# High and low parts of the last 64 attention rows formed at the scaling of the units; a new order of the end; the first block's combinations in two sections

## The chip, the cores and the metric

The kernel runs on one core of one Trainium2 chip. The core has five engines that this document speaks of by the profile's names: PE (TensorE, matrix products; PEld is its weight load), DVE (VectorE), ACT (ScalarE), POOL (GpSimd) and SP (SyncE), which here only issues DMAs. The metric is the time of one execution on the device in microseconds, the median of the runs. Lower is better.

## The reference

A transformer-like block with a gate. S = 2048 tokens, D = 576, 32 heads of 18, F = 4608, all in float32:

```python
def _A_ref(x, wqkv, wo):                     # attention
    qkv = (x @ wqkv).reshape(B, S, 3, H, Dh).transpose(2, 0, 3, 1, 4)
    q, k, v = qkv[0], qkv[1], qkv[2]
    p = _softmax(jnp.einsum("bhqd,bhkd->bhqk", q, k) * (Dh ** -0.5), axis=-1)
    o = jnp.einsum("bhqk,bhkd->bhqd", p, v)
    return o.transpose(0, 2, 1, 3).reshape(B, S, D) @ wo

def _B_ref(x, w_gate, w_up, w_down):         # feed-forward
    return (_gelu(x @ w_gate) * (x @ w_up)) @ w_down

x = A_x
xn = _layernorm(x, axis=-1)
s = _A_ref(xn, A_wqkv, A_wo)
g = _silu(_B_ref(xn, B_w_gate, B_w_up, B_w_down))
return x + s * g
```

## The kernel before

**High and low parts.** Matrix products that have to be accurate are made of two reduced-precision parts of each operand: `hi` is the value rounded to the matmul's type, `lo` is what is left (`cut`, lines 436 to 441). A product then takes three matmuls: hi times hi, hi times lo, lo times hi.

**Sections.** The feed-forward part is cut into 144 sections, S0 to S143: for each of 4 blocks of 512 tokens, 18 groups r of 256 hidden columns, in two halves. A section is 27 pairs of matmuls (gate and up, L412). Into 128 sections the attention is spliced: scores for the row maxima (`pm`, L780, reduced on DVE, L782), scores again and their exponentials (`pe`, L832, and ACT L833), and the sums of values (`acc`, L849). Small pieces of work for other engines hang on a section's pair numbers as hooks. The splits of the next section's weights (`wh`, `wl`, L110 and L112, three pairs of instructions on POOL) are made while a section runs.

**Downs.** After the two halves of a group comes a down projection, `down`: seven products of a Strassen-like scheme into PSUM tiles `py` (L523), of which DVE adds each to one of seven sums M in SBUF (L530). The tiles pg/pu, pm, pe, py and po of PE share a few PSUM buffers (`ring`: three), so PE waits where an older tile isn't read yet. The weight operand T of a down (high and low, seven slots each) is formed on chip once and stored; later downs load it in four pieces (`t_piece`, 576 and 432 KB). For the first group of a block M is not added to but copied: on DVE for the second block (L526), on ACT for the third and fourth (L528). After a block's last down the seven sums are combined in four pairs of in-place operations (`COMBINED`, L542), and four of them, the block's quarters, are stored to `ys` (L549).

**Attention's outputs** are scaled in 32 units u = 8j + g (token block j, head group g): a unit is loaded, multiplied by the reciprocals of its sums on POOL (L693) and stored to `on[j]`, 576 rows, in four DMAs (L700).

**The end.** The 576 attention rows are projected with `wo` in 16 steps of 128 tokens. A step k is `project` (28 matmuls, L1006), `multiply` (the gate and the sum with x, L1015 to L1020, and the store L1021) and `split_o(k + 2)`, which forms the operands of a later step: `oh` on ACT from all five row groups (128x640, L989), `ol` on DVE from the first four (L990), and for the last 64 rows their low part on DVE into the upper half of `oh`'s fifth slot (L991). The fifth slot then holds high rows over low rows. `split_wo` forms `wo`'s two parts, `woh` on ACT (L968) and `wol` on POOL (L966, L970). The raw `wo` lies in the tiles xx and yy, which later hold rows of x and of y. The attention rows of a block lie in KA (`load_o`: 1024 KB, L718, and 128 KB, L719). The last sections are mixed with the steps by hand. D0, D1 and D2 are the last three downs (`last_down`):

```python
# order on PE: S139, S140, S141, D0, steps 0 to 3, S142, steps 4 to 6, D1, step 7, S143,
#              steps 8 to 10, D2, step 11, gates of the last block with steps 12, then 13 to 15
```

**What sets the order.** PE's and SP's instructions stand in the order of the code in the whole program. SP issues its DMAs one after the other, and one that waits for its source or for its buffer holds up those behind it. On ACT, DVE and POOL a scheduler sets the order, up to the end, from where on (`manual_schedule`) it is that of the code too. Each engine takes its instructions in that order.

Of the kernel before, what the change touches and what calls it, by code (L numbers as in the profile page):

```python
# [8 lines left out]
F32 = mybir.dt.float32  # L9
F32R = mybir.dt.float32r  # L10
# [55 lines left out]
def f(ap):  # L66
    return ap.bitcast(F32)
# [15 lines left out]
def kernel(ctx: ExitStack, tc: tile.TileContext, x, wqkv, wo, w_gate, w_up, w_down, out):  # L83
# [12 lines left out]
    rT = dram.tile([H, S], F32, name="rT")  # L96
    on = [dram.tile([D, TB], F32, name=f"on{b}") for b in range(NB)]
    mxT = [dram.tile([8 * QD, P], F32, name=f"mxT{i}") for i in range(2)]
# [5 lines left out]
    ident = const.tile([P, P], F32, name="ident")  # L104
    make_identity(nc, ident)
    all_t = slice(0, TB)

# [406 lines left out]
    def down(b, r, then={}):  # L514
        if b == 0 and r < PLAIN:
            return down_plain()
        (ah, al), T, M = FF["A"], FF["T"], FF["M"]
        for m, (i, k) in PRODUCTS:
            py = ring("py")
            for t in range(2):  # L520
                tt = slice(t * P, (t + 1) * P)
                for n, (h, w) in enumerate(((ah, 0), (ah, 1), (al, 0))):
                    nc.tensor.matmul(py[:, t, 0:DC], h[:, i, tt], T[:, w, k], start=n == 0, stop=n == 2)  # L523
            if r == 0:
                if b == 1:
                    nc.vector.tensor_copy(M[:, m], py[:, :, 0:DC])  # L526
                else:
                    nc.scalar.activation(M[:, m], py[:, :, 0:DC], AF.Copy)  # L528
            else:
                nc.vector.tensor_tensor(M[:, m], py[:, :, 0:DC], M[:, m], op=ALU.add)  # L530
            for eng, to, op, by in then.get(m, ()):
                eng.tensor_tensor(M[:, to], M[:, to], M[:, by], op=op)
        if r == NR - 1 and b < NB - 1:
            FF["gates"].append(b)
            one = nc.vector if b == 0 else nc.gpsimd
            for i, p, q in COMBINED:
                FF["hooks"].setdefault(i, []).append(lambda p=p, q=q: (combine(one, *p), combine(nc.gpsimd, *q)))

    def combine(eng, to, op, by):

        M = FF["M"]
        tc.keep_in_program_order(eng.tensor_tensor(M[:, to], M[:, to], M[:, by], op=op))  # L542

    def gates():

        for b in FF["gates"]:
            for i, c, m in QUARTERS:
                rows = slice(b * TB + TH * i, b * TB + TH * i + TH)
                nc.sync.dma_start(ys[rows, DC * c:DC * c + DC].rearrange("(t p) d -> p t d", p=P), FF["M"][:, m])  # L549
        FF["gates"] = []  # L550
# [139 lines left out]
    def scale(u, i):  # L690

        o, d = (t[:, i, 0:TB] for t in SC)
        nc.gpsimd.tensor_tensor(o, o, d, op=ALU.mult)  # L693

    def store_scale(u, i):

        j, g = divmod(u, NQ)
        for a in range(QD):
            row = (QD * g + a) * DH
            nc.sync.dma_start(on[j][row:row + DH, :], SC[0][32 * a + 1:32 * a + 1 + DH, i, 0:TB])  # L700

# [13 lines left out]
    def load_o(b):  # L715

        i = OTS[b]
        nc.sync.dma_start(f(KA)[:, i:i + KT], on[b][0:R0, :].rearrange("(k p) t -> p k t", p=P))  # L718
        nc.sync.dma_start(f(KA)[0:HR, i + KT], on[b][R0:D, :])  # L719

    ctx.enter_context(tc.manual_schedule(engines={mybir.EngineType.SP}))

    with tc.tile_pool(name="att", bufs=1, reuse_waits="tile") as att:
        VS = [att.tile([P, VC * VW + 32 - DH - 1], F32, name=f"VS{i}") for i in range(VB)]
        for i, kk in enumerate(KS):
            for r in range(2):
                (nc.vector, nc.gpsimd)[i % 2].memset(f(kk[r]), 1.0)
# [218 lines left out]
    with tc.tile_pool(name="epi", bufs=1, reuse_waits="tile") as epi:  # L946
# [37 lines left out]
        def split_o(k):  # L984
            if k < len(groups):
                b, j = groups[k]
                oh, ol = OP[k] = [epi.tile([P, c, P], F32R, name=m, bufs=2) for m, c in (("oh", NK), ("ol", KT))]
                raw = f(KA)[:, OTS[b]:OTS[b] + NK, j * P:(j + 1) * P]
                act.activation(oh, raw, AF.Copy)  # L989
                vec.tensor_tensor(ol, raw[:, 0:KT], f(oh)[:, 0:KT], op=SUB)  # L990
                vec.tensor_tensor(oh[HR:P, KT, :], raw[0:HR, KT], f(oh)[0:HR, KT, :], op=SUB)  # L991

        def gate(k):
            if gated <= k < len(groups) and groups[k][0] < NB - 1:
                yy = YY[k % len(YY)]
                th = epi.tile([P, D], F32, name="th")
# [3 lines left out]
        def project(k):  # L1000
            po = ring("po")
            oh, ol = o = OP.pop(k)
            terms = [(c, i, w) for c in range(KT) for i, w in ((0, 0), (0, 1), (1, 0))] + [(KT, 0, 0), (KT, 0, 1)]
            for c in range(2):
                for m, (i, a, w) in enumerate(terms):
                    nc.tensor.matmul(po[:, c, 0:DC], o[a][:, i, :], OW[w][:, i, DC * c:DC * c + DC], start=(m == 0),  # L1006
                                     stop=(m == len(terms) - 1))
            return po
# [13 lines left out]

        def step(ahead=True):
            nonlocal n
            multiply(n, project(n))
# [10 lines left out]
            if ahead:  # L1036
                gate(n + 1)

# [3 lines left out]
        def last_section(tag):  # L1042
# [16 lines left out]
            t1 = h[:, 0:2].rearrange("p a t -> p (a t)")  # L1059
            act.activation(t1, pg, AF.Square)  # L1060
            vec.scalar_tensor_tensor(t1, t1, 1.0 / GC, pg, op0=ADD, op1=ALU.mult)
            act.activation(t1, t1, AF.Tanh, scale=GC * GS)

            def end():
# [3 lines left out]
            return h, end  # L1068

# [9 lines left out]
        load_raw(first + 2)  # L1079
        h, end = last_section("f")  # L1080
        todo.pop("rec")[0]()
# [10 lines left out]
        h, end = last_section("ring")  # L1092
# [12 lines left out]
        end()  # L1105
        gate(0)
        gate(1)
        sums_a(0, h, pool)
# [10 lines left out]
        for k in range(3, len(XX)):  # L1119
            load_x(k)  # L1120
        for k in range(4):
            step()
        h, end = last_section("ring")
        end()
        for k in range(2):
            step()
        step(False)
        last_down(1)
        gate(n + 1)
        sums_a(0, h, pool)  # L1130
        cut_a(0, h, pool, pool)
        step()
        h, end = last_section("f")
        end()
        sums_a(1, h, vec)
        cut_a(1, h, act, vec)
        for k in range(2):
            step()
        step(False)
        last_down(2, {6: ((vec, 6, SUB, 3),), 0: ((vec, 6, ADD, 0), (pool, 5, ADD, 0), (pool, 5, ADD, 2)),  # L1140
                      4: ((vec, 6, SUB, 4), (vec, 4, ADD, 2)), 1: ((pool, 5, SUB, 1), (pool, 1, SUB, 3))})
        step()
        M = FF["M"]
        for i, c, m in QUARTERS:
            t = ffn.tile([P, 2, DC], F32, name="tg", tag=("h0", "h1")[c], bufs=2 - c)
            act.activation(t, M[:, m], AF.Tanh, scale=0.25)
            vec.scalar_tensor_tensor(M[:, m], t, 1.0, M[:, m], op0=ADD, op1=ALU.mult)
            if m == 4:
                step()
        for k in range(3):  # L1150
            step()
# [28 lines left out]
```

## Time and profile before

| | us |
|---|---|
| median of 3 runs | 2583.61 (2580.03 to 2584.37) |
| the profiled execution's own time | 2580.15 |
| its span, first to last instruction | 2578.4 |
| PE busy | 2545.5 (99%) |
| DVE busy | 2105.1 (82%) |
| POOL busy | 1630.5 (63%) |
| ACT busy | 1464.1 (57%) |

The rows of the trace are to be read so. A row of a timeline is: start and duration in us, engine, line, operation, output and inputs, shapes, count; in square brackets is the engine's idle time just before and what ended it. The chain of waits lists, in order of time, the pieces of work that decide the end: start, duration, engine, what, line. A row of the stretches gives for each engine its busy time and the number of its instructions, then the granted clock of PE (1.00 is full), the mean busy share of the 16 DMA engines and the rate in GB/s. All numbers below are of the one profiled execution.

### The profile page before, as it was taken

Reading aid. Unit: us, or ns where it says so; the run is one execution under the profiler, and the core shown is the slowest. Engines: PE = TensorE matmul, PEld = TensorE weight load, DVE = VectorE, ACT = ScalarE, POOL = GpSimd, SP = SyncE. Lnnn points to the kernel's source line nnn. Section 1 sums busy time; section 2 is a strip of 40 time slices with the busy share of each in tenths; the row PEclk is TensorE's granted clock in tenths of the full one; section 3 lists DMA queues with packets and bytes.
Section 4 is the critical chain, followed back from the end, with each engine's and each line's share of the span. In section 5 each row is a group of like instructions: output and inputs, shape, how many; then the busy total and the mean of one; then the engine's idle time right before and its main releaser. Section 6 shows DMA issues by size and latency. Waiting matters only on the chain.

```text
span 2578.4 us, 52876 instructions
## 1 busy us (share of the span) xinstructions
PE 2545.5 (99%) x20548; PEld 1838.7 (71%) x20548; DVE 2105.1 (82%) x2383; ACT 1464.1 (57%) x1765; POOL 1630.5 (63%) x1692
## 2 busy tenths in 40 slices
PE   9999999999999999999999999999999999999988
PEld 8888766676766676666667766666776766666787
DVE  5325888888889888888888888889887888897467
ACT  3224366666666655555666555656656556666621
POOL 2105588888888856566658566666657566666662
PEclk9999999999999999999999999999999999999999
DMA  8854455555575566666686666666668656665684
GB/s 259 270 187 131 104 165 163 163 166 167 163 197 177 164 157 163 166 162 166 169 195 182 168 172 168 167 164 170 166 162 210 165 159 165 165 164 148 174 264 138
DMA packets 409769, 446.43 MB, mean 173 GB/s; under 512 B 106924, under 2 KB 286636, under 8 KB 409520
## 3 DMA queue, kind: packets, MB, share of 16 engines
q1 hardware_dynamic: 409520, 443.04, 62.8%
q8 instruction: 164, 2.69, 0.5%
q14 instruction: 85, 0.70, 0.1%
HBM read 347.07 MB, written 95.85 MB: 172 GB/s over the span
## 4 chain that ended last, share of the span: by engine, by line
PE 95%; DVE 3%; DMA 1%; ACT 1%; POOL 1%; issue 0%; SPq 0%; DVEq 0%; POOLq 0%; ACTq 0%
PE pg L412 26%; PE acc L849 18%; PE py L523 15%; PE pm L780 9%; PE pe L832 9%; PE pu L412 8%; PE po L189 7%; PE po L1006 1%; PE py L510 1%; PE pt L250 0%; DVE mx L782 0%; DMA yy<-in_A_wo_dram 0%; DVE ol L990 0%; DVE M L530 0%; DMA od<-rT 0%
## 5 line engine op out<-in xcount | busy, mean ns | idle before, releaser
L833 ACT ACTIVATE pT<-pe 128x1024 f32<-128x1024 f32 x1024 | 1047.7, 1027 | 578.0 <-PE pe L832 542.6
L782 DVE TENSOR_REDUCE mx<-pm 128x2 f32<-128x1024 f32 x1024 | 1220.9, 1224 | 167.5 <-PE pm L780 151.9
L412 PE MATMUL pu<-xd,wh 64*128 64x512 f32 x2538 | 925.6, 396 | 1.6 <-DVE t L426 1.6
L412 PE MATMUL pg<-xd,wh 64*128 64x512 f32 x2538 | 924.8, 396 | 1.9 <-ACT t L425 1.9
L412 PEld LDWEIGHTS pg<-xd,wh 64*128 64x128 f32 x2538 | 467.7, 184 | 122.4 <-issue 57.9
L412 PE MATMUL pg<-xd,wl 64*128 64x512 f32 x1269 | 495.4, 390 | 1.2 <-POOL wl L117 1.2
L412 PE MATMUL pu<-xd,wl 64*128 64x512 f32 x1269 | 495.1, 390 | 0.0
L412 PEld LDWEIGHTS pu<-xd,wh 64*128 64x128 f32 x2538 | 467.5, 184 | 20.4 <-DVE t L426 2.9
L849 PE MATMUL acc<-pT,VS 128*32 128x512 f32 x4096 | 466.0, 595 | 0.0
L110 POOL TENSOR_SCALAR wh<-raw 128x384 fp32r<-128x384 f32 x402 | 215.9, 539 | 381.4 <-PE pu L412 272.5
L112 POOL TENSOR_TENSOR wl<-raw,wh 128x384 fp32r<-128x384 f32 x402 | 414.1, 1032 | 28.4
L780 PE MATMUL pm<-KA,QT 64*128 64x512 f32 x2048 | 414.1, 394 | 4.6 <-ACT pT L833 2.8
L832 PE MATMUL pe<-QT,KA 64*128 64x512 f32 x2048 | 410.1, 392 | 3.3 <-DVE mx L782 3.3
L523 PE MATMUL py<-T,ah 128*128 128x288 f32 x1876 | 382.8, 299 | 7.6 <-DVE M L530 7.5
L530 DVE TENSOR_TENSOR M<-py,M 128x576 f32<-128x576 f32 x448 | 338.7, 758 | 30.4 <-PE py L523 17.6
L523 PEld LDWEIGHTS py<-T,ah 128*128 128x128 f32 x1876 | 299.8, 189 | 62.5 <-issue 54.0
L441 POOL TENSOR_TENSOR al<-h,ah 128x512 fp32r<-128x512 f32 (+1 forms) x142 | 292.5, 2060 | 52.6 <-ACT ah L438 42.4
L849 PEld LDWEIGHTS acc<-pT,VS 128*32 128x32 f32 x4096 | 120.2, 109 | 276.6 <-issue 229.6
L523 PE MATMUL py<-T,al 128*128 128x288 f32 x938 | 276.5, 295 | 0.0
L832 PEld LDWEIGHTS pe<-QT,KA 64*128 64x128 f32 x2048 | 192.7, 184 | 113.8 <-DVE mx L782 28.4
L412 PEld LDWEIGHTS pg<-xd,wl 64*128 64x128 f32 x1269 | 234.0, 184 | 37.4 <-POOL wl L117 2.0
L412 PEld LDWEIGHTS pu<-xd,wl 64*128 64x128 f32 x1269 | 234.2, 185 | 9.6
(163 smaller groups left out, 2925.4 us busy)
## 6 DMA issues: line engine op xcount, KB each, us to landing
T<-ts SPq DMA_DIRECT2D x98, 576.0 KB
KA<-qk SPq DMA_DIRECT2D x768, 72.0 KB
T<-ts SPq DMA_DIRECT2D x98, 432.0 KB
raw<-in_B_w_gate_dram SPq DMA_DIRECT2D x144, 288.0 KB
raw<-in_B_w_up_dram SPq DMA_DIRECT2D x144, 288.0 KB
ts<-T SPq DMA_DIRECT2D x36, 576.0 KB
VS<-vs SPq DMA_DIRECT2D x128, 152.0 KB
qk<-t SPq DMA_DIRECT2D x72, 256.0 KB
```

The source lines that it names most:

```text
L110: first = nc.gpsimd.tensor_scalar(hi, raw, 1.0, 1.0, op0=ALU.mult, op1=ALU.mult)
L112: keep(nc.gpsimd.tensor_tensor(lo, raw, f(hi), op=ALU.subtract))
L189: nc.tensor.matmul(o, st, m, start=(i == 0), stop=(i == len(terms) - 1))
L412: nc.tensor.matmul(o, w[1 + wp][k][rr, c, :], xd[k][xp][rr, c, :], start=(i == 0), stop=(i == len(terms) - 1))
L441: keep(two.tensor_tensor(lo, raw, f(hi), op=ALU.subtract))
L523: nc.tensor.matmul(py[:, t, 0:DC], h[:, i, tt], T[:, w, k], start=n == 0, stop=n == 2)
L530: nc.vector.tensor_tensor(M[:, m], py[:, :, 0:DC], M[:, m], op=ALU.add)
L780: nc.tensor.matmul(pm[:, a], QS[u, r][rr, t * P:(t + 1) * P], KS[(u * NA + c) % KB][r][rr, :], start=True, stop=True)
L782: return nc.vector.tensor_reduce(MX[u][:, 2 * r:2 * r + 2, t, c], pm, axis=AX.X, op=ALU.max)
L832: nc.tensor.matmul(pe[:, a], KS[(u * NA + c) % KB][r][rr, t * P:(t + 1) * P], QS[u, r][rr, :], start=True, stop=True)
L833: nc.scalar.activation(PT[u, kt][:, 2 * r:2 * r + 2, :], pe, AF.Exp, scale=SCALE)
L849: nc.tensor.matmul(ACC[u][32 * a:32 * a + 32, :], VS[(u * NA + c) % VB][:, v:v + 32], pt[:, a, :], start=first, stop=last, skip_group_chec ...
```

## The change

It has four parts.

1. **The last 64 rows.** `on[j]` gets 640 rows. In the units that hold the last 64 attention rows (g = 7, four of 32) POOL forms their high part, with a mask `split_rows` that is 0 for the rows of the first 512, and subtracts it (L706 and L707 of the changed kernel). Nine DMAs store high and low rows one after the other, where four stored the rows. `load_o` then brings the fifth slot with both parts, 256 KB for 128 KB, and `project` reads it from KA. `split_o` forms four groups only: ACT 128x512 for 128x640, and L991 is gone.
2. **The first block.** Its four pairs of combinations, which stood in the one section after the block's last down, are spread: one in that section, three in the next; its stores to `ys` go later too. The seven copies of M for the second block go from DVE to ACT.
3. **The order of the end.** PE's order becomes S139, S140, S141, D0, steps 0 to 2, S142, 3 to 5, D1, S143, 6 to 8, D2, 9 to 15. `split_wo` and `split_o(1)` are issued behind D0. The gelu of a section (all of it) is issued in one piece after it or after the first step behind it. In the half `cut_a(1)` of S143 the low part goes from DVE to POOL.
4. **Loads and shares.** `load_o(2)` and `load_o(3)` are issued with steps 3 and 7, where they were issued with 1 and 5. POOL takes the addition of x in odd steps below 8, before below 11.

The core of the diff:

```diff
-SHARED = 11
+SHARED = 8
-COMBINED = ((6, (6, ADD, 0), (5, ADD, 0)), (12, (6, SUB, 3), (5, ADD, 2)), (18, (6, SUB, 4), (5, SUB, 1)),
-            (24, (4, ADD, 2), (1, SUB, 3)))
+COMBINED = (((6, ADD, 0), (5, ADD, 0)), ((6, SUB, 3), (5, ADD, 2)), ((6, SUB, 4), (5, SUB, 1)), ((4, ADD, 2), (1, SUB, 3)))
...
             if r == 0:
-                if b == 1:
-                    nc.vector.tensor_copy(M[:, m], py[:, :, 0:DC])
-                else:
-                    nc.scalar.activation(M[:, m], py[:, :, 0:DC], AF.Copy)
+                nc.scalar.activation(M[:, m], py[:, :, 0:DC], AF.Copy)
...
-            for i, p, q in COMBINED:
-                FF["hooks"].setdefault(i, []).append(lambda p=p, q=q: (combine(one, *p), combine(nc.gpsimd, *q)))
+            if b == 0:
+                combine_at(14, nc.vector, *COMBINED[0])
+            else:
+                for k in range(4):
+                    combine_at(6 * k + 6, nc.gpsimd, *COMBINED[k])
...
+            if b == 0:
+                for i, k in ((2, 1), (8, 2), (13, 3)):
+                    combine_at(i, nc.vector, *COMBINED[k])
+                FF["hooks"].setdefault(20, []).append(lambda b=b: store_gates(b))
+            else:
+                store_gates(b)
...
         nc.gpsimd.tensor_tensor(o, o, d, op=ALU.mult)
+        if u % NQ == NQ - 1:
+            nc.gpsimd.tensor_scalar(d.bitcast(F32R), o, split_rows, 1.0, op0=ALU.mult, op1=ALU.mult)
+            nc.gpsimd.tensor_tensor(o, o, d, op=SUB)
...
-        nc.sync.dma_start(f(KA)[0:HR, i + KT], on[b][R0:D, :])
+        nc.sync.dma_start(f(KA)[:, i + KT], on[b][R0:R0 + P, :])
...
-                vec.tensor_tensor(ol, raw[:, 0:KT], f(oh)[:, 0:KT], op=SUB)
-                vec.tensor_tensor(oh[HR:P, KT, :], raw[0:HR, KT], f(oh)[0:HR, KT, :], op=SUB)
+                vec.tensor_tensor(ol, raw, f(oh), op=SUB)
...
-            b, j = groups[min(n + 2, len(groups) - 1)]
+            b, j = groups[n]
             if b < 2 and j == TB // P - 1:
                 load_o(b + 2)
...
+        h1, gelu = last_section("f")
+        last_down(0)
         split_wo()
-        split_o(1)
         for k in range(3):
             load_x(k)
         for k in range(2, 4):
             load_y(k)
-        h1, end = last_section("f")
-        last_down(0)
-        end()
-        gate(0)
-        gate(1)
+        split_o(1)
+        gelu()
...
         last_down(1)
-        gate(n + 1)
         sums_a(0, h, pool)
         cut_a(0, h, pool, pool)
+        h, gelu = last_section("f")
+        gelu()
+        sums_a(1, h, vec)
+        for k in range(3):
+            step()
+            if k == 0:
+                cut_a(1, h, act, pool)
+        last_down(2, {0: ((pool, 5, ADD, 0), (pool, 5, ADD, 2)),
...
-        h, end = last_section("f")
-        end()
-        sums_a(1, h, vec)
-        cut_a(1, h, act, vec)
-        for k in range(2):
-            step()
-        step(False)
```

Three places show what moves.

POOL between S140 and D0, before: the scaling of the last two units, `wol`, and then the three splits of S142's weights (raw_31111), of which the first stands last here.

```order
L693 TENSOR_TENSOR on_11642<-on_11642,od_11643 128x512 x2
L966 MEMSET wol_31010 64x576
L970 TENSOR_TENSOR wol_31010<-xx0_31011,woh_31009 128x576
L970 TENSOR_TENSOR wol_31010<-xx1_31012,woh_31009 128x576
L970 TENSOR_TENSOR wol_31010<-xx2_31013,woh_31009 128x576
L970 TENSOR_TENSOR wol_31010<-yy2_31016,woh_31009 128x576
L970 TENSOR_TENSOR wol_31010<-yy3_31017,woh_31009 64x576
L110 TENSOR_SCALAR wh_31232<-raw_31111 128x384
L112 TENSOR_TENSOR wl_31233<-raw_31111,wh_31232 128x384
```

And now (raw_31140 are S142's raw weights; a third pair L110, L112 stands between the last row of the first part and the first of the second):

```order
L704 TENSOR_TENSOR on_11653<-on_11653,od_11654 128x512 x2
L706 TENSOR_SCALAR od_11654<-on_11653,split_rows_87 128x512
L707 TENSOR_TENSOR on_11653<-on_11653,od_11654 128x512
L110 TENSOR_SCALAR wh_31249<-raw_31140 128x384
L112 TENSOR_TENSOR wl_31250<-raw_31140,wh_31249 128x384
L110 TENSOR_SCALAR wh_31253<-raw_31140 128x384
L112 TENSOR_TENSOR wl_31254<-raw_31140,wh_31253 128x384
```

and, behind that third pair,

```order
L991 MEMSET wol_31042 64x576
L995 TENSOR_TENSOR wol_31042<-xx0_31043,woh_31041 128x576
L995 TENSOR_TENSOR wol_31042<-xx1_31044,woh_31041 128x576
L995 TENSOR_TENSOR wol_31042<-xx2_31045,woh_31041 128x576
L995 TENSOR_TENSOR wol_31042<-yy2_31048,woh_31041 128x576
L995 TENSOR_TENSOR wol_31042<-yy3_31049,woh_31041 64x576
```

All of `wol` now stands behind the three splits, and each of these reads S142's raw weights.

SP from step 6's end on, before: step 7's store is that of xx0_31011, step 8's that of xx1_31012, and the load of KA for the last block (on3_72) has gone after step 5.

```order
L1021 DMA out_0_dram<-xxs_31372 128x576
L978 DMA yy2_31016<-ys_75 128x576
L982 DMA xxs_31372<-in_A_x_dram 128x576
L1021 DMA out_0_dram<-xx0_31011 128x576
L468 DMA T_1911<-ts_77 128x1152
L468 DMA T_1911<-ts_77 128x864
L978 DMA yy3_31017<-ys_75 128x576
L982 DMA xx0_31011<-in_A_x_dram 128x576
L1021 DMA out_0_dram<-xx1_31012 128x576
L468 DMA T_1911<-ts_77 128x1152
L468 DMA T_1911<-ts_77 128x864
```

And now: step 6's store is that of xxs_31409, step 7's that of xx0_31043.

```order
L1047 DMA out_0_dram<-xxs_31409 128x576
L468 DMA T_1912<-ts_77 128x1152
L468 DMA T_1912<-ts_77 128x864
L1003 DMA yy2_31048<-ys_75 128x576
L1007 DMA xxs_31409<-in_A_x_dram 128x576
L1047 DMA out_0_dram<-xx0_31043 128x576
L740 DMA KA_1913<-on3_72 128x4x512
L741 DMA KA_1913<-on3_72 128x512
L468 DMA T_1912<-ts_77 128x1152
L468 DMA T_1912<-ts_77 128x864
```

The load of KA (1024 and 256 KB) now stands between the two halves of T, and both it and T's second half stand behind the store of step 7.

DVE in the section after the first block's last down and at the start of the next, before (L782 are the reductions of the maxima, L422 to L429 the first section's gelu):

```order
L542 TENSOR_TENSOR M_1908<-M_1908 128x576
L782 TENSOR_REDUCE mx_8414<-pm_9156 128x2
L782 TENSOR_REDUCE mx_8414<-pm_9172 128x2
L542 TENSOR_TENSOR M_1908<-M_1908 128x576
L782 TENSOR_REDUCE mx_8414<-pm_9194 128x2
L542 TENSOR_TENSOR M_1908<-M_1908 128x576
L782 TENSOR_REDUCE mx_8414<-pm_9210 128x2
L782 TENSOR_REDUCE mx_8414<-pm_9226 128x2
L542 TENSOR_TENSOR M_1908<-M_1908 128x576
L782 TENSOR_REDUCE mx_8414<-pm_9244 128x2
L422 SCALAR_TENSOR_TENSOR h1_9254<-h1_9254,pg_9100 128x512
L426 TENSOR_TENSOR t2_9257<-t2_9257,pg_9100 128x512
```

with no combination in the section behind. And now in the section behind, while one combination is left in the first:

```order
L905 RECIPROCAL sums_8833<-sums_8833 128x16
L807 TENSOR_REDUCE mx_9327<-pm_9328 128x2
L544 TENSOR_TENSOR M_1909<-M_1909 128x576
L807 TENSOR_REDUCE mx_9327<-pm_9347 128x2
L544 TENSOR_TENSOR M_1909<-M_1909 128x576
L827 STREAM_TRANSPOSE mt_9362<-m2_9275 128x32
L807 TENSOR_REDUCE mx_9327<-pm_9366 128x2
L807 TENSOR_REDUCE mx_9327<-pm_9385 128x2
L544 TENSOR_TENSOR M_1909<-M_1909 128x576
```

Of four combinations on DVE three have moved behind the gelu of the first section, in among the next section's reductions. On POOL their partners moved likewise, the last one behind the three sums that form `tsum` (L475 to L477).

More of the change, by code (lines that the diff above doesn't have):

```diff
@@ L96 @@
     rT = dram.tile([H, S], F32, name="rT")
-    on = [dram.tile([D, TB], F32, name=f"on{b}") for b in range(NB)]
+    on = [dram.tile([R0 + P, TB], F32, name=f"on{b}") for b in range(NB)]
     mxT = [dram.tile([8 * QD, P], F32, name=f"mxT{i}") for i in range(2)]
@@ L724 @@
         VS = [att.tile([P, VC * VW + 32 - DH - 1], F32, name=f"VS{i}") for i in range(VB)]
+        nc.gpsimd.memset(split_rows, 1.0)
+        for c in range(1 + R0 % DH):
+            nc.gpsimd.tensor_tensor(split_rows, split_rows, ident[:, c:c + 1], op=SUB)
         for i, kk in enumerate(KS):
@@ L1021, in multiply, with step @@
             nc.sync.dma_start(out[rows(k), :], xx)
-        def step(ahead=True):
+        def step():
             nonlocal n
-            multiply(n, project(n))
+            po = project(n)
+            multiply(n, po)
             split_o(n + 2)
-            b, j = groups[min(n + 2, len(groups) - 1)]
+            b, j = groups[n]
             if b < 2 and j == TB // P - 1:
@@ L1091 @@
         split_o(0)
-        h, end = last_section("ring")
-        end()
+        h, gelu = last_section("ring")
+        gelu()
         for i, u in enumerate(rest):
@@ L1147 @@
             vec.scalar_tensor_tensor(M[:, m], t, 1.0, M[:, m], op0=ADD, op1=ALU.mult)
-            if m == 4:
+            for k in range({6: 1, 4: 2}.get(m, 0)):
                 step()
-        for k in range(3):
+        for k in range(2):
             step()
```

71 lines of the change are left out of this document (41 added, 30 removed).

## The prediction

> **What bounds the kernel now.** I read the page's busy times first, then in the timeline of PE the rows that end its idle times, then the chain of waits back from the longest.
>
> ```profile
> PE 2545.5 (99%) x20548; PEld 1838.7 (71%) x20548; DVE 2105.1 (82%) x2383; ACT 1464.1 (57%) x1765; POOL 1630.5 (63%) x1692
> ```
>
> PE is the bound: idle 32.9 us of a span of 2578.4. The change takes no matmul away, so all it can win or lose are waits of PE. Those at its places:
>
> ```profile
> 761.24 0.50 PE L832 MATMUL pe<-QT,KA 64*128 64x512 f32 x2 [1.03 <-DVE mx L782]
> 765.28 0.50 PE L832 MATMUL pe<-QT,KA 64*128 64x512 f32 x2 [1.21 <-DVE mx L782]
> 767.73 0.50 PE L832 MATMUL pe<-QT,KA 64*128 64x512 f32 x2 [1.03 <-DVE mx L782]
> 2476.19 0.85 PE L523 MATMUL py<-T,ah 128*128 128x288 f32 x2 [5.58 <-DVE M L530]
> 2491.45 0.40 PE L1006 MATMUL po<-woh,oh 128*128 128x288 f32 x1 [1.12 <-DVE oh L991]
> 2518.88 0.53 PE L523 MATMUL py<-T,ah 128*128 128x288 f32 x2 [1.26 <-DVE M L530]
> 2542.35 0.40 PE L1006 MATMUL po<-woh,ol 128*128 128x288 f32 x1 [2.05 <-DVE ol L990]
> 2549.45 0.53 PE L523 MATMUL py<-T,ah 128*128 128x288 f32 x2 [0.66 <-DVE M L530]
> 2562.18 0.40 PE L1006 MATMUL po<-woh,ol 128*128 128x288 f32 x1 [1.25 <-DVE ol L990]
> ```
>
> The idle time before a row stands in its brackets, with what ended it. Three rows at the first change of blocks, 3.27 us, behind DVE; six at the end, 5.58 + 1.12 + 1.26 + 2.05 + 0.66 + 1.25 = 11.9 us. Where the 5.58 comes from, the chain of waits tells:
>
> ```profile
> 2461.44 8.69 DMA yy<-in_A_wo_dram
> ...
> 2471.56 1.79 DVE ol L990
> ...
> 2476.19 5.12 PE py L523 x24
> 2481.31 3.73 PE po L1006 x28
> ...
> 2518.88 3.47 PE py L523 x24
> ```
>
> `split_o(1)` stands ahead of D0's additions on DVE and waits for `wo`. The 24 matmuls after the stall took 5.12 us, after the short wait at 2518.88 as many took 3.47: a restart after a long wait costs 1.65 more.
>
> **The change, part by part.** Work that no wait of PE hangs on: two POOL instructions and five more DMAs in each of four units lie in idle time of POOL (37% of the span) and of SP, except at the end, where POOL's are counted. The nearest rows for them:
>
> ```profile
> L440 POOL TENSOR_SCALAR ah<-h 128x512 fp32r<-128x512 f32 x2 | 1.7, 835 | 2.0 <-PE py L523 1.9
> L441 POOL TENSOR_TENSOR al<-h,ah 128x512 fp32r<-128x512 f32 x2 | 2.6, 1284 | 0.2
> ```
>
> 2.1 us together. ACT, which gets the shorter split, is busy 57%.
>
> *The end of D0 and step 0.* With `split_o(1)` behind D0 the 5.58 goes, and PE is at step 0 at 2470.61 + 24 x 0.133 (3.73/28) = 2473.8. What is late next is `wol`, which step 0's second matmul reads.
>
> ```profile
> 2448.20 0.63 SPq L130 DMA_DIRECT2D raw<-in_B_w_up_dram  x1
> 2454.06 0.52 POOL L110 TENSOR_SCALAR wh<-raw 128x384 fp32r<-128x384 f32 x1 [0.63 <-DMA raw<-in_B_w_up_dram]
> 2467.96 0.64 SPq L130 DMA_DIRECT2D raw<-in_B_w_up_dram  x1
> 2467.98 0.58 POOL L966 MEMSET wol<- 64x576 f32 x1
> 2468.64 4.17 POOL L970 TENSOR_TENSOR wol<-xx,woh 128x576 fp32r<-128x576 f32 x3
> 2475.99 0.51 POOL L110 TENSOR_SCALAR wh<-raw 128x384 fp32r<-128x384 f32 x1
> 2480.69 0.74 POOL L447 TENSOR_TENSOR h<-h 128x256 f32<-128x256 f32 x1
> ```
>
> Now the three splits stand ahead, and wait for S142's weights, issued as before up to 2467.96. The load of S141's took 5.9 us from issue (2448.20) to the split that waited for it (2454.06); as much here gives 2473.9. It is 2475.99 at the latest, where the split began without a wait; and POOL isn't through with the scaling before 2467.9 (where the memset began) + 2.1 = 2470.0. I take 2473.9. Splits 2480.69 - 2475.99 = 4.7, memset 0.66, `wol` 2475.99 - 2468.64 = 7.35: the first part of `wol` is there at 2480.6, the last at 2486.6, and step 0 needs some 15 more matmuls (2.0, and 15/24 of the 1.65 for a restart, 1.0): its end is 2489.6 against 2485.04. **+4.6**; from the two bounds -0.4 to +7.3.
>
> ```profile
> 2479.00:2480.00 1.00, 1.00 (x6) 1.00 (x6) 0.52 (x1) 0.00 (x0) 0.92 (x3) 0.54 0.89 244
> 2480.00:2481.00 1.00, 1.00 (x9) 1.00 (x9) 0.68 (x2) 0.00 (x0) 1.00 (x2) 1.00 0.98 332
> ```
>
> These stretches show the restart: the granted clock (before the DMA share) is still 0.54 in the fourth us after the stall, then 1.00. The Trainium skill (TensorE: Matmul & The Clock Gate, Part 1: The HAM clock gate) says that full clock comes back only after about 3.4 us of sustained activity; the trace agrees for a dense restart. By that rule step 0, which would get a few matmuls each time a part of `wol` is formed, would not count as busy, and some of step 1 would run slowly too: up to 0.7 more than my 1.0. No row shows such a drip.
>
> *The waits after it.* L991 is gone, D0's additions stand ahead of the splits and nothing new stands ahead of the later ones: 1.12 + 1.26 + 2.05 + 0.66 + 1.25 = **-6.3**. If one of the larger stays for another reason, -4.
>
> *D2.* Its second matmul reads T's second half. In the chain at S143:
>
> ```profile
> 2532.41 0.05 PE pg L412
> ...
> 2537.44 1.28 ACT ah L438
> L441 POOL TENSOR_TENSOR al<-h,ah 128x1280 fp32r<-128x1280 f32 x1 | 3.2, 3246 | 0.1
> L1020 POOL TENSOR_TENSOR xx<-xx,yy 128x576 f32<-128x576 f32 x3 | 5.6, 1867 | 23.3 <-DVE yy L1015 22.3 <-DMA xxs<-in_A_x_dram 1.0
> PEld py L523 <- DMA T<-ts: 0.3, 1, 0.3
> 2542.11 0.93 SPq L468 DMA_DIRECT2D T<-ts  x2
> 2497.00:2503.00 6.00, 6.00 (x53) 4.90 (x53) 2.86 (x3) 0.74 (x1) 4.34 (x5) 1.00 1.03 355
> 2542.00:2546.00 4.00, 3.65 (x27) 3.61 (x27) 3.89 (x6) 0.00 (x0) 1.82 (x1) 1.00 0.84 268
> ```
>
> S143 ends at 2532.47, its high part is ready 6.25 us later. POOL then makes the low part (3.25), and its addition of x in step 7 stands behind that (1.87): step 7's store can go 11.4 us after S143. PE is through its three steps after 3 x 3.73 = 11.2. SP issues behind that store the load of KA and only then T's second half. Bytes up to T's first needed piece: 288 + 1024 + 256 + 576 KB, 2.2 MB, at 355 GB/s (the stretch where KA was loaded) 6.2 us. The pair of pieces issued at 2542.11, 1.03 MB, was through at about 2546, 3.9 us, of which 2.9 are its bytes at that rate: about 1 us from issue to the first bytes. Landing 11.4 + 0.3 + 6.2 + 1.0 = 18.9 after S143. PE waits **7.7**, and 1.65 for its restart: **+9.3**. The lower bound: the piece isn't held up by KA. Then it is issued 12.7 after S143 (KA's two issues and the store's before it) and has the 3.9 us: 16.6, a wait of 5.4. The upper bound has everything at 268 GB/s and T's whole pair waited for, 2.6 MB in 9.8 us: 11. With the restart 5 to 13. I take the first, since the piece stands in the one queue of SP right behind KA, and 16 engines busy 1.03 in that stretch leave it no free way. The Trainium skill (DMA: Bandwidth & Descriptors, Queues, rings and completion order) has it that each DMA engine takes one issuer's descriptors in order; by this the piece comes behind KA and the wait is the 7.7, without it the 5.4. No row here has a piece of T close behind a load of KA.
>
> *The first block.*
>
> ```profile
> L528 ACT ACTIVATE M<-py x14: 651/652/654, 1387.8 to 1992.8; 128x576 f32<-128x576 f32 x14
> L542 DVE TENSOR_TENSOR M<-M x4: 1200/1408/1847, 758.6 to 768.7; 128x576 f32<-128x576 f32 x4
> 768.50:782.50 14.00, 14.00 (x122) 8.78 (x120) 13.60 (x17) 10.06 (x12) 12.00 (x14) 1.00 0.90 257
> 788.20 0.80 POOL L477 TENSOR_TENSOR tsum<-rawd 128x288 f32<-128x288 f32 x1
> 789.93 1.17 ACT L483 ACTIVATE T<-tsum 128x1152 fp32r<-128x1152 f32 x1 [4.73 <-PE py L523]
> 793.29 1.94 ACT L833 ACTIVATE pT<-pe 128x1024 f32<-128x1024 f32 x2 [0.34 <-PE pu L412]
> ```
>
> The first section loses three of four combinations on DVE: of its 3.27 some 2.1 go, or all. The second section had 13.60 of 14.00 us of DVE busy, one combination of 1.20 in it; with three (median 1.41, 4.2) it has 16.6, so PE waits about 2.5 (1.0 if what DVE carried over shrinks with the first section, 3.9 if they take 1.85). DVE's seven copies behind it go to ACT, 7 x 0.65 = 4.6 us. ACT had 4.73 idle, but now waits: M1's last combination stands on POOL behind the sums ending 789.0, its store follows it (789.0 + 1.4 + 0.8 for 288 KB and 1 to start: 792 at best, 793 with what stands in SP's queue), and only then may M1 be copied; the exponentials that began at 793.29 stand behind that copy, L483 and two more splits, at about 796.6. PE has three buffers; I take 2.5 of these 3.3, bounds 0 and 3.3. Sum -2.1 + 2.5 + 2.5 = **+2.9**; -2.3 to +5.1.
>
> Sum: 4.6 - 6.3 + 9.3 + 2.9 = **+10.5** on 2580.15, 2590.7. That execution lies at the lower end of the runs, 3.5 below their median; on the median it would be 2594.1. I forecast 2593.
>
> **Rivals.** (a) D2 doesn't wait. For it: in before T's pieces were waited for once, 0.3 us, and a load of KA moves only 128 KB more than before. Against it: the order on SP and POOL. It decides at 11.2 us after S143, and 9.3 falls away: +1.2, 2581 on the profiled execution. This one ends on the other side, not slower. (b) The weights land early and the block change pays: step 0 at -0.4 and the blocks at -2.3, with D2 as forecast: +0.3, 2580. Against it stands the load of 5.9 us. Only (a) and (b) together are faster: -9, 2571. (c) The change doesn't do what it says: the later waits stay in part and the bounds of step 0 and D2 lie high: -4 + 7.3 + 13 + 2.9 = +19, 2599 (2603 on the median).
>
> **How the numbers follow.** Forecast, +5.2 to +15: 0.68; (c) 0.13; (a) 0.08 and (b) 0.05, of which a part still falls outside 0.2%; both 0.06. A measurement of this kernel can tell about 0.2%, 5.2 us, from no change. Slower 0.82, same 0.11, faster 0.07. The range runs from (a) and (b) on the median, 2584, less a little, to (c): 2583 to 2603.
>
> **What would show it.** Right: no wait at the first matmuls of D0's third product, a wait of some 7 us at step 0's second matmul ended by POOL `wol`, and one of some 8 at D2's first product ended by the DMA of T; new waits behind DVE in 770 to 785 and behind ACT after 787. Wrong: `wol` before 2474, or T's second half landing before D2.

## The result and the profile after

The changed kernel takes 2599.7 us in the median of 4 runs (2598.63 to 2600.66), the one before 2583.29 in the runs beside them. The ratio is 1.0066, with a 95% interval of 1.0048 to 1.0083: slower, by 12 to 21 us.

The page of the changed kernel, its busy times and its chain by engine:

```profile
PE 2553.1 (98%) x20548; PEld 1846.2 (71%) x20548; DVE 2083.8 (80%) x2360; ACT 1465.4 (56%) x1772; POOL 1642.1 (63%) x1710
PE 92%; POOL 2%; DMA 2%; DVE 1%; issue 1%; ACT 1%; SPq 0%; POOLq 0%; DVEq 0%; ACTq 0%
```

The matmuls are as many. The span of the profiled execution is 2598.9, 20.5 longer than that of before, with 12.9 us more idle time of PE (2598.9 - 2553.1 against 32.9) and 7.6 more in which it was busy, at a lower clock as will be seen. DVE has 21 us less to do, and POOL and DMA hold 2% of the chain each, where they held 1%. The rows of PE's timeline in the changed kernel that end a wait, at the first change of blocks, at step 0, at D2 and behind it:

```profile
763.22 0.50 PE L857 MATMUL pe<-QT,KA 64*128 64x512 f32 x2 [0.65 <-DVE mx L807]
775.59 0.50 PE L857 MATMUL pe<-QT,KA 64*128 64x512 f32 x2 [0.47 <-DVE mx L807]
778.91 0.50 PE L857 MATMUL pe<-QT,KA 64*128 64x512 f32 x2 [0.48 <-DVE mx L807]
791.01 0.53 PE L523 MATMUL py<-T,ah 128*128 128x288 f32 x2 [2.57 <-ACT M L525]
792.80 0.85 PE L523 MATMUL py<-T,ah 128*128 128x288 f32 x2 [0.74 <-ACT M L525]
2489.94 0.61 PE L1032 MATMUL po<-wol,oh 128*128 128x288 f32 x1 [9.39 <-POOL wol L995]
2491.30 0.61 PE L1032 MATMUL po<-wol,oh 128*128 128x288 f32 x1 [0.27 <-POOL wol L995]
2548.57 0.37 PE L523 MATMUL py<-T,ah 128*128 128x288 f32 x1 [0.89 <-DMA T<-ts]
2557.91 0.61 PE L523 MATMUL py<-T,ah 128*128 128x288 f32 x1 [8.97 <-DMA T<-ts]
2575.53 0.40 PE L1032 MATMUL po<-woh,ol 128*128 128x288 f32 x1 [1.62 <-DVE ol L1015]
```

The six waits of the end that the prediction summed are gone, the 5.58 of D0 among them. In their place stand 9.39 at step 0 (and four more of 0.27 or 0.28), 0.89 and 8.97 at D2, and one of 1.62.

**Step 0.** POOL's timeline of the changed kernel, the end of the scaling, the first split of S142's weights, and `wol`; SP's issue of these weights ahead of it:

```profile
2475.43 0.63 SPq L130 DMA_DIRECT2D raw<-in_B_w_up_dram  x1
2476.09 1.31 POOL L707 TENSOR_TENSOR on<-on,od 128x512 f32<-128x512 f32 x1
2483.09 0.51 POOL L110 TENSOR_SCALAR wh<-raw 128x384 fp32r<-128x384 f32 x1 [5.68 <-DMA on<-on]
2487.84 0.57 POOL L991 MEMSET wol<- 64x576 f32 x1
2488.49 4.11 POOL L995 TENSOR_TENSOR wol<-xx,woh 128x576 fp32r<-128x576 f32 x3
2492.56 2.77 POOL L995 TENSOR_TENSOR wol<-yy,woh 128x576 fp32r<-128x576 f32 x2
```

POOL is idle for 5.68 us with `wol` waiting behind the split. The weights were there 7.7 us after their issue. The releaser named is a store of a scaled unit, but POOL waits here for the weights: by the trace's records of landings twelve of the sixteen parts of the load were there by 2480.81 and the last at 2482.91, and POOL's wait for them ends at 2482.93. The nine stores were being issued meanwhile; what held up the last four parts is not shown.

**D2.** SP in the changed kernel: the store of step 7, the load of KA, T's second half; and the piece of the chain of waits that it starts:

```profile
2548.08 0.34 SPq L1047 DMA_DIRECT2D out_dram<-xx  x1
2548.46 0.43 SPq L740 DMA_DIRECT2D KA<-on  x1
2549.51 1.21 SPq L468 DMA_DIRECT2D T<-ts  x2
2549.51 8.36 DMA T<-ts
2557.91 8.33 PE py L523 x41
```

S143 ended at 2536.36 (step 6's first matmul stands at 2536.29); the store goes 11.7 us after that, the piece lands after 21.5.

**The first block.** POOL's last combination, the copies on ACT, and the stores to `ys` on SP, in the changed kernel:

```profile
788.87 1.40 POOL L544 TENSOR_TENSOR M<-M 128x576 f32<-128x576 f32 x1
786.16 0.65 ACT L525 ACTIVATE M<-py 128x576 f32<-128x576 f32 x1 [2.36 <-PE py L523]
790.30 0.65 ACT L525 ACTIVATE M<-py 128x576 f32<-128x576 f32 x1 [3.49 <-POOL M L544]
799.02 2.85 ACT L858 ACTIVATE pT<-pe 128x1024 f32<-128x1024 f32 x3
781.19 9.98 SPq L550 DMA_DIRECT2D ys<-M  x4
```

The second copy waits 3.49 us for POOL's last combination (M1 less M3). The row does not name the sum that it writes; M1's product is the last of the seven, so it can only be M3, which the combination reads. The exponentials begin at 799.0, where they began at 793.3. Set beside each other matmul by matmul, the two traces say what this cost: the changed kernel is 0.2 us ahead as the first section begins, 3.4 after it, 1.4 after the second section, and 5.5 us behind once the down and the section after it are through.

### The profile page after: what moved, and what is told of

Same layout as the page of the kernel before. It is cut to its first block, busy times and chain, and to the rows that moved or that the text cites. A ratio compares the mean times of both kernels' runs of the same rounds, so it can differ in the third digit from the quotient of the medians.

```text
span 2598.9 us, 52905 instructions
## 1 busy us (share of the span) xinstructions
PE 2553.1 (98%) x20548; PEld 1846.2 (71%) x20548; DVE 2083.8 (80%) x2360; ACT 1465.4 (56%) x1772; POOL 1642.1 (63%) x1710
## 4 chain that ended last, share of the span: by engine, by line
PE 92%; POOL 2%; DMA 2%; DVE 1%; issue 1%; ACT 1%; SPq 0%; POOLq 0%; DVEq 0%; ACTq 0%
PE pg L412 21%; PE acc L874 17%; PE py L523 14%; PE pu L412 11%; PE pe L857 9%; PE pm L805 9%; PE po L189 7%; PE po L1032 2%; PE py L510 1%; DMA raw<-in_B_w_up_dram 1%; DVE mx L807 0%; DMA od<-rT 0%; PE pt L250 0%; DMA T<-ts 0%; POOL wl L112 0%
## 5 line engine op out<-in xcount | busy, mean ns | idle before, releaser
L110 POOL TENSOR_SCALAR wh<-raw 128x384 fp32r<-128x384 f32 x402 | 215.5, 539 | 385.1 <-PE pu L412 262.7
L112 POOL TENSOR_TENSOR wl<-raw,wh 128x384 fp32r<-128x384 f32 x402 | 416.9, 1039 | 27.7
```

The lines of the kernel that those rows point to most:

```text
L110: first = nc.gpsimd.tensor_scalar(hi, raw, 1.0, 1.0, op0=ALU.mult, op1=ALU.mult)
L112: keep(nc.gpsimd.tensor_tensor(lo, raw, f(hi), op=ALU.subtract))
```

## The experiments

All are compared with the kernel before in runs on the same chip. Where a difference from the changed kernel is given, it is taken from its 2599.7; before's median was 2583.29 beside that and 2581.72, 2580.89 and 2582.42 beside the three sets of experiments, so such a difference can be off by 1 to 2.5 us.

**The first block alone, and all but it.** The kernel before with part 2 of the change, and the changed kernel without it:

```diff
-            one = nc.vector if b == 0 else nc.gpsimd
-            for i, p, q in COMBINED:
...
+            if b == 0:
+                combine_at(14, nc.vector, *COMBINED[0])
...
-                if b == 1:
-                    nc.vector.tensor_copy(M[:, m], py[:, :, 0:DC])
...
+                nc.scalar.activation(M[:, m], py[:, :, 0:DC], AF.Copy)
```

> The kernel before with the changed first block alone (one combination pair in the first section, three in the next, the stores to ys later, the seven copies on ACT). Theory: the whole loss that the trace after shows between 754 and 802 us comes from this part and no other: it falls from 0.2 us ahead to 3.4 ahead in the first section, gives 1.9 back in the second, and 6.9 in the down behind, where the copy of M3 on ACT waits for POOL's last combination, which reads M3. So 5.7 us slower than before, 2589. Rival: part of that loss belongs to the other parts (the longer stores of the scaled units, the moved loads), and this part alone costs the 2.9 of the prediction or less, 2586.

2586.52 against 2581.72, ratio 1.0018 (1.0010 to 1.0027): 4.8 us slower. The trace has the same waits at the same places (2.57 and 0.74 at the down).

> The changed kernel with the first block as before (four combination pairs in one section, copies on DVE). Theory: 5.7 us come back, 2594, and the end is as slow as in the changed kernel, some 14 us behind before. Rival: the loss at the first block is 2.9 by its own, so 2597.

2594.82 against 2581.72, ratio 1.0050 (1.0038 to 1.0063): 13.1 us slower. So the two parts add, 4.8 + 13.1 = 17.9 where the whole change costs 16.4. The time alone does not rule out the rival of 2.9 for the first block, since the interval of that run goes from 2.6 to 7.0 us. Its trace does: set beside that of before it is 1.1 us ahead as the first section begins and 5.2 behind once the down and the section after it are through.

**`wol` ahead of the splits.**

```diff
+        split_wo()
         h1, gelu = last_section("f")
         last_down(0)
-        split_wo()
```

> The changed kernel with the forming of wo's parts issued ahead of the splits of S142's weights, as before the change; D0's additions still stand ahead of the splits of the attention rows. Theory: the 9.4 us wait at step 0 and the slow clock after it are owed to that order alone: wol then follows POOL's scaling directly (its end at 2477.4, seven and a half us long), step 0 ends some 12 us earlier, and D2's wait stays as it is: 2588. Rival: the wait is owed to the late load of the weights itself; then S142 waits for its splits instead, and no more than 5 us are won: 2595.

2589.94, ratio 1.0030 (1.0018 to 1.0041): 9.8 us faster than the changed kernel. PE's timeline of this kernel at step 0 and D2:

```profile
2481.59 0.40 PE L1032 MATMUL po<-wol,oh 128*128 128x288 f32 x1 [0.70 <-POOL wol L995]
2483.40 0.61 PE L1032 MATMUL po<-wol,oh 128*128 128x288 f32 x1 [1.15 <-POOL wol L995]
2549.67 0.61 PE L523 MATMUL py<-T,ah 128*128 128x288 f32 x1 [10.48 <-DMA T<-ts]
```

The 9.39 is owed to the order on POOL. What is left at step 0 is the time that POOL takes for `wol` itself. D2's wait is even longer.

**T's pieces for D2 directly behind D1.**

```diff
         cut_a(0, h, pool, pool)
+        for t in pieces:
+            t()
+        del pieces[:]
         h, gelu = last_section("f")
```

> The changed kernel with the four pieces of T for D2 issued directly behind D1 instead of with steps 6 and 7. Theory: D2's wait of 8.97 us is owed to the place of the pieces behind the store of step 7 and the load of KA; it goes, with the slow clock behind it, 11 us in all: 2589. Rival: D2 then waits for the low part of S143's half on POOL, or step 12 for the rows of the last block, which are loaded after T as before; half of it comes back: 2594.

2587.14, ratio 1.0020 (1.0011 to 1.0030): 12.6 us faster than the changed kernel. D2 has one wait of 0.54 left, behind DVE. KA, now loaded behind T, is not waited for.

**The loads of KA as before.**

```diff
-            b, j = groups[n]
+            b, j = groups[min(n + 2, len(groups) - 1)]
```

> The changed kernel with the loads of the rows of blocks 2 and 3 issued with steps 1 and 5 as before; T's pieces stay with steps 6 and 7. Theory: T's second half then stands behind the store of step 7 alone, 11.7 us after S143; by what the queue moves it lands some 4 us earlier, so D2 waits 5 in place of 9.9: 5 us faster than the changed kernel, 2594.5. Rival: KA's bytes have no part in it and the store's lateness has all: 2599.

2594.62, ratio 1.0049 (1.0036 to 1.0062): 5.1 us faster than the changed kernel, as expected. PE and SP in this kernel:

```profile
2547.22 0.34 SPq L1047 DMA_DIRECT2D out_dram<-xx  x1
2547.61 0.91 SPq L468 DMA_DIRECT2D T<-ts  x2
2548.13 0.37 PE L523 MATMUL py<-T,ah 128*128 128x288 f32 x1 [1.31 <-DMA T<-ts]
2552.71 0.61 PE L523 MATMUL py<-T,ah 128*128 128x288 f32 x1 [4.21 <-DMA T<-ts]
```

So the wait at D2 has two parts: with the load of KA out of the way T's second half comes 5.1 us after its issue instead of 8.4; what remains is the place behind the store of step 7.

**The copies alone, and the spreading alone**, each on the kernel before.

> The kernel before with the seven copies of M for the second block on ACT in place of DVE, its combinations all in the one section as before. Theory: the copies cost nothing by themselves; the 6.9 us lost in that down are owed to the copy of M3, which must wait for POOL's last combination because that reads M3, and here the combinations are long done. Within 1 us of before. Rival: the copies hold up ACT's split of T's high part and the exponentials behind it, 2.5 us as the prediction priced it, or more: 2584 to 2586.

2581.93 against 2580.89, ratio 1.0002 (0.9994 to 1.0011): no difference. One new wait of 1.32 behind ACT stands in its trace after the down. There the trace falls from 1.4 us ahead of before to level with it; of these 1.4 only 0.5 were won at this change of blocks.

> The kernel before with the combinations spread over two sections and the stores later, the copies on DVE as before. Theory: the copy of M3 waits for POOL's last combination on DVE as it does on ACT; the sections give 1.2 us (3.2 won, 1.9 lost) and the down takes some 4 to 6: 3 to 5 us slower than before. Rival: the loss belongs to the copies on ACT; then only the 1.2 are seen, faster than before.

2586.19, ratio 1.0022 (1.0013 to 1.0031): 5.3 us slower, as much as the two together. DVE's copies in that kernel:

```profile
785.00 0.76 DVE L525 COPY M<-py 128x576 f32<-128x576 f32 x1 [0.33 <-PE py L522]
789.14 0.76 DVE L525 COPY M<-py 128x576 f32<-128x576 f32 x1 [3.39 <-POOL M L546]
```

The wait for POOL's last combination is the same on DVE as on ACT. By these times it is the spreading that costs, not the engine that copies.

**The last combination on DVE.** The changed kernel with M1 less M3 taken from POOL:

```diff
-    def combine_at(i, eng, p, q):
-        FF["hooks"].setdefault(i, []).append(lambda: (combine(eng, *p), combine(nc.gpsimd, *q)))
+    def combine_at(i, eng, p, q, other=None):
+        FF["hooks"].setdefault(i, []).append(lambda: (combine(eng, *p), combine(other or nc.gpsimd, *q)))
...
-                    combine_at(i, nc.vector, *COMBINED[k])
+                    combine_at(i, nc.vector, *COMBINED[k], nc.vector if k == 3 else None)
```

> The changed kernel with one instruction moved: the last combination (M1 less M3) goes from POOL, where it stands behind the three sums of tsum, to DVE. Theory: the copy of M3 no longer waits, the down behind loses little, while DVE's full section loses 1 us more: 5 us faster than the changed kernel, 2594.5. Rival: M5's copy still waits for the store of M5, which goes last and late; no more than 2 us are won.

2602.85, ratio 1.0082 (1.0069 to 1.0096): 3 us slower than the changed kernel (5.6, if each is taken against its own runs of before). The expectation fell, both ways of it. DVE and PE:

```profile
783.53 1.05 DVE L544 TENSOR_TENSOR M<-M 128x576 f32<-128x576 f32 x1 [5.62 <-POOL M L544]
785.77 0.79 PE L857 MATMUL pe<-QT,KA 64*128 64x512 f32 x2 [7.18 <-DVE mx L807]
798.70 0.53 PE L523 MATMUL py<-T,ah 128*128 128x288 f32 x2 [0.74 <-ACT M L525]
```

The copies no longer wait for POOL (the 2.57 is gone), but the moved instruction does: M5 less M1 on POOL must read M1 first, POOL is busy with the splits until then, and DVE's reductions of maxima queue behind it.

**POOL's combinations left in place, DVE's spread**, on the kernel before.

```diff
+                for k in range(4):
+                    combine_at(6 * k + 6, nc.gpsimd, COMBINED[k][1])
+                combine_at(14, nc.vector, COMBINED[0][0])
...
+                    combine_at(i, nc.vector, COMBINED[k][0])
```

> The kernel before with DVE's four combinations spread over two sections as in the change, POOL's four left in the first section, the copies on DVE. Theory: what the spreading lost, it lost by POOL's combinations coming behind its busy stretch, so that copies, and DVE, wait for POOL; left in place they cost nothing and the two sections give their 1 to 2 us: 2580, 5 us faster than with all eight spread. Rival: the late stores to ys are the cause, the copies of M1 and M5 wait for them here too: some 4 us slower than before.

2584.93 against 2582.42, ratio 1.0010 (1.0001 to 1.0019): 2.5 us slower, between the two, with an interval (0.3 to 4.9 us) that reaches the rival. The trace decides. The copies wait for POOL no more, so that cause stands. The stores go in the later section here too, and no copy waits for them, so they aren't it; the down still loses 1.6 us, with one wait of 0.85 behind DVE's copies. But the one combination in the first section takes 3.88 us on DVE, and PE waits 3.25 behind it:

```profile
760.57 3.88 DVE L548 TENSOR_TENSOR M<-M 128x576 f32<-128x576 f32 x1
760.45 1.45 POOL L493 TENSOR_TENSOR T<-rawd,T 128x576 fp32r<-128x576 f32 x1
761.85 1.41 POOL L548 TENSOR_TENSOR M<-M 128x576 f32<-128x576 f32 x1
763.23 0.62 POOL L439 TENSOR_SCALAR ah<-h 128x512 fp32r<-128x512 f32 x1
765.64 0.79 PE L847 MATMUL pe<-QT,KA 64*128 64x512 f32 x2 [3.25 <-DVE mx L797]
```

**The last rows alone**, on the kernel before: `split_rows`, the stores, the load of 128 rows, and `project` reading them; the end's order and all loads as before.

> The kernel before with the last 64 rows alone changed: their parts formed at the scaling, the fifth slot loaded with both, L991 gone; the end's order as before. Theory: L991 stands in the chain of D0's wait (1.39) and of the wait at 2490.33 (1.12), so some 2.5 to 4 us are won, 2578. Rival: DVE's place in those chains is taken by the next instruction, and five more DMAs a unit cost as much: no change.

2578.8 against 2582.42, ratio 0.9984 (0.9976 to 0.9993): 3.6 us faster. The 5.58 at D0 is 4.91 there, the 1.12 behind L991 is gone, and the 1.26 ahead of D1 is 0.54.

**The end mended.** The changed kernel with the first block as before, `wol` ahead of the splits, and T's pieces behind D1.

> The changed kernel's end and last rows with the first block as before, wo's parts ahead of the splits of S142's weights and the pieces of T for D2 directly behind D1. Theory: the three losses are independent and add: 2599.7 - 4.8 (block) - 9.8 - 12.6 = 2572.5, some 9 us faster than before. Rival: with the wait at step 0 gone the steps come earlier on the loads behind them, and part of it comes back at D1 or at the steps that wait for KA: 2577 to 2580.

2572.1 against 2580.89, ratio 0.9965 (0.9953 to 0.9978): 8.8 us faster than the kernel before, and 0.4 from the sum (1.2, if each loss is taken against its own runs of before). It is the fastest of the versions run.

**One step further.** Beyond that, `wol` between the scalings of the last two units, D2's combinations behind the next step, and DVE's combinations of the first block spread:

```diff
             scale(u, i)
             store_scale(u, i)
+            if i == 0:
+                split_wo()
...
```

> A version made of what the runs showed: end_mended with wo's low parts between the scalings of the last two units, D2's combinations behind the step after it, and DVE's combinations of the first block spread with POOL's left in place. Theory: against end_mended's 2572.1 the waits left at step 0 (2.5 and a slow clock of 1.5), the 1.6 before step 9's successor and 1 to 2 at the first block go: 2567. Rival: POOL's scaling of the last unit and the splits of S142's weights then come late for S142, and the combinations late for the gates; 2572 as before.

2579.41 against 2582.42, ratio 0.9993 (0.9984 to 1.0002): what end_mended had won is nearly gone. `wol` is early, step 0 has no wait; but the last unit's scaling and with it its nine stores are late, and the loads of x stand behind these on SP. DVE waits for x, with a split of a later step behind it:

```profile
2487.93 1.58 DVE L1051 TENSOR_TENSOR xx<-xx,yy 128x576 f32<-128x576 f32 x1 [6.40 <-DMA xx<-in_A_x_dram]
2491.24 0.61 PE L1037 MATMUL po<-woh,ol 128*128 128x288 f32 x1 [7.34 <-DVE ol L1020]
```

Two smaller losses stand beside it in this trace: D2's first matmul waits 2.29 us for T, and the first change of blocks loses 2.6 us, where DVE's combinations are spread as in the run above with POOL's left in place.

## Why the prediction was right, and where its sum was short

The direction, the three places and the engines behind each wait came as forecast, and the time lies inside the range. The sum was 10.5 us and the runs gave 16.4, which is above the +5.2 to +15 to which the prediction gave 0.68. Term by term, from the traces:

- **Step 0, +4.6 forecast.** Step 0's product is read at 2499.26 in the changed kernel and at 2485.06 before; the changed kernel was 6.6 behind on coming there (5.5 from the first block, 0.9 in one section at 983 whose weights came late, a loss that only the trace of the spreading alone has too, the rest in crumbs). That leaves 7.6, just beyond the upper bound of 7.3. (By the sum itself, its two starts of 2470.0 and 2475.99 give +0.7 and +6.7, not -0.4 and +7.3.) What was mis-sized most is the load of the weights: 5.9 us taken, 7.7 measured. They were also issued 0.9 later than taken, and `wol` took 6.8 where 7.35 was taken. The other part is the clock. Granted clock by stretches of the changed kernel (columns as before):

```profile
2490.00:2492.00 2.00, 1.73 (x6) 1.38 (x6) 0.00 (x0) 0.00 (x0) 2.00 (x2) 0.50 0.49 128
2496.00:2498.00 2.00, 2.00 (x10) 2.00 (x10) 0.00 (x0) 0.00 (x0) 1.83 (x3) 0.50 0.82 265
2498.00:2500.00 2.00, 2.00 (x14) 2.00 (x14) 0.74 (x1) 0.63 (x1) 2.00 (x4) 0.77 1.09 201
2500.00:2502.00 2.00, 2.00 (x18) 2.00 (x17) 1.97 (x3) 0.00 (x0) 1.91 (x3) 1.00 1.05 253
```

While PE gets three matmuls for each part of `wol` its clock stays at 0.50, though the row shows it busy for 1.73 of 2 us, and it is 1.00 only some 3.5 us after the last such wait (2495.38): the mean of 0.77 from 2498 to 2500 puts the change near 2498.9. The prediction gave the rule of the Trainium skill (TensorE: Matmul & The Clock Gate, Part 1: The HAM clock gate), by which full clock needs some 3.4 us of sustained activity, up to 0.7 us more than it took itself. The trace agrees with the rule: the 71 matmuls from 2495.38 on took 11.38, where 84 of a dense stretch took as long, 1.75 us lost against the 1.0 taken.

- **The waits after it, -6.3 forecast.** All five went. One came that the prediction didn't have: 1.62 behind DVE at 2573.91, where D2's combinations now all stand after the last product and the split for a later step behind them. By the waits alone that is -4.7. But a wait costs more than its own length: against a step without a wait (3.87) and a down without one (5.74) the five places took some 8.0 us more before, and the new one takes 1.9. So -6.1; that it comes near the forecast is chance, since two things left out cancel.
- **D2, +9.3 forecast.** The store of step 7 went 11.7 us after S143, forecast 11.4; PE was there after 11.3, forecast 11.2. The piece landed later than taken: after 21.5, forecast 18.9. When KA was issued, at 2548.46, the queue still had T's first half to move, issued late itself, and two loads of rows of y and x (by the records of landings they were there by 2549.6 and 2551.0); the sum left them out, and the 0.89 is the wait for that first half. The restart cost 2.7 us in place of 1.65 (41 matmuls in 8.33, 42 in 5.74 in a dense down). In all 12.6, about what the run with T's pieces moved gave back (12.6, or 11.0 if each is taken against its own runs of before). The forecast's lower bound with the restart is 7 by its own 5.4 and 1.65, not 5. That the piece comes behind KA was the choice between two ways; the run with KA loaded early settles it (8.97 and 4.21), and in the changed kernel KA's two loads had landed by 2556.2, T's piece behind them at 2557.87. The trace so agrees with the Trainium skill's rule that each DMA engine takes one issuer's descriptors in order (DMA: Bandwidth & Descriptors, Queues, rings and completion order).
- **The first block, +2.9 forecast.** First section -3.2 for -2.1; second +1.9 for +2.5; the down +6.9 for +2.5. The step that failed is this last: the prediction let the copy of M1 wait for its store. The copy that waits is an earlier one, at 790.30, for POOL's last combination itself; of the four combinations POOL has, that one reads M3, which the copy overwrites. PE then has no free buffer for 2.57 and 0.74 us and waits 0.56 more at 798.27, and the exponentials come 5.7 us later, forecast 3.3. The sum also had no slow clock here, and there was one, worth some 1.4 us (pairs of matmuls take 0.85 and 0.68 behind the second wait, 0.43 ahead of it):

```profile
793.00:795.00 2.00, 2.00 (x9) 2.00 (x10) 0.00 (x0) 0.64 (x2) 0.84 (x2) 0.50 0.55 172
```

The last 1.6 of the 6.9 lie around these waits and are not taken apart. And it isn't ACT: the copies alone cost nothing that can be told.

Together with the 0.9 at 983 that is 7.6 - 6.1 + 12.6 + 5.7 + 0.9 = 20.7, against 20.5 between the two profiled executions. Of the rivals, (a) fell at D2's wait, (b) at both of its terms, and (c), with the higher bounds, came nearest in size, though its later waits did not stay. That the added work of part 1 costs nothing held; the run of part 1 alone is even 3.6 us faster, since L991 no longer stands in the chains of the waits, and the prediction had booked that among the waits that go.

## What to carry to other kernels

Before a piece of work is moved ahead of another in an engine's queue, look at what the moved piece itself waits for: all that stands behind it then waits as long, and a load that was never on the path is on it. Here a load issued early cost nothing that showed, and one behind the store of a late result cost 11 to 12.6 us: put loads in the one queue where their buffer comes free, not where the step that uses them is written. When in-place operations are spread out to relieve an engine, the last one to read each buffer decides when that buffer can be written again, so the engine that runs it must be free by then.

## What the runs showed of the hardware that was not expected

An addition of two 128x576 operands in SBUF took DVE 3.88 us beside POOL's two additions one behind the other, where the same operation took 0.74 to 1.28 at other places of the changed kernel. By the Trainium skill (SBUF — State Buffer, Who interferes with whom) a DVE instruction with two SBUF inputs and a GpSimd one that reads SBUF share a port that one of them holds for its whole instruction. The trace agrees as far as it goes: DVE ends at 764.45, after POOL's second addition (763.26) and the short instruction behind it (763.85). That DVE was passed over more than once is read from these rows, not tried by itself.

The clock did not come back while PE was busy most of the time in small groups of matmuls (0.50 at 1.73 of 2 us busy). And what a wait costs in slow matmuls behind it is no fixed share of its length: 2.7 us behind 8.97, 1.65 behind 5.58, some 1.4 behind the 2.57 and 0.74 of the first block. It is about half of the time for which PE then worked at 0.50, which by the clock records of the traces was 5.9, 3.7 and 2.9 us. Between the start and the end of the fourteen traces every stretch at 0.50 lasts 3.41 us or a whole multiple of it (6.83, 13.65, once 17.07), so a short wait can cost nearly as much behind it as a longer one.
